# A fused attention and mixture kernel on one core: sums over keys brought into token order by overlapping tiles and a block transpose on VectorE, with other edits

## The chip, the cores and the metric

The kernel runs on one core of a Trainium2 chip. The metric is device time in microseconds, the median of several runs of the whole program; lower is better.

## The reference

Three stages follow each other. Attention over 4 batches of 8 heads with 1152 keys and 64 columns a head; the queries are first averaged in pairs, so that 576 are left:

```python
q_pool = q.reshape(B, H, S // 2, 2, D).mean(axis=3)
attn = softmax(q_pool @ k.T / sqrt(D))          # over the 1152 keys
x = (attn @ v)                                  # 2304 tokens x 512
```

Then a soft mixture of 8 experts with 4 slots each, and at the end a two-layer block:

```python
logits = x @ phi                                # 2304 x 32
d = softmax(logits, over tokens); c = softmax(logits, over slots)
slot_out[e] = relu((d.T @ x)[e] @ w1[e]) @ w2[e]
x = c @ slot_out
h = x @ w_in
out = piecewise(h) @ w_out     # h above 1, (h+1)^2/4 between, 0 below -1
```

## The kernel before

**Attention.** Two heads are worked on together, which makes 16 pairs (P, `NP`), four to a batch. The keys of a pair are 9 chunks of 128 (`NK`). A step g is one chunk of one pair (g = 9 P + c), and each step has two halves, h = 0 and 1, one for each head. In one half the loop at the end of the attention part issues, in this order:

- `max_half`: scores of another pair, 11 chunks ahead, with the queries on the partitions (tile `mx`, 4 matmuls in float16, L297), of which VectorE takes the largest (L309).
- `st`: the scores of this chunk with the keys on the partitions (tile `st`, 4 matmuls with `K` and 4 with `S`, L363), of which ScalarE takes the exponential (tile `e`, L368).
- at the first half of some steps, what `pre` holds: `es_sum` of the pair that has just ended (L387), and before it `t_pe` of an older pair (L422, L430).
- `pv`: values times exponentials of the chunk before, 4 matmuls in float32 instructions (tile `acc`, L394).
- `slot(g, h)`: whatever the schedule `sched` holds for this half: sums, evictions, preparation of later pairs, conversion of weights.

`mx`, `st` and the tiles of the steps in token order (`tx`, `lt`, `lr`, `pb`) share one ring of three PSUM buffers (`sc_tile`, tag `sc`). A matmul into a buffer waits until the last reader of what the buffer held is done: VectorE if that was an `mx`, ScalarE if it was an `st`.

**The sums over keys.** `es_add` adds the exponentials of chunks 0 to 5 on VectorE (L376, whole 128x576 tiles or half ones, by the table `ADD`: half-step, chunk, head, first and last part). `es_sum` then multiplies the sum and the chunks 6 to 8 with a column of ones repeated 32 times, into free columns of `acc`, in columns 0 to 191 and 192 to 287 of each query half. At b + 9 (b = 9 P) `t_raw` and `t_sum` copy `acc` to `xT` and the sums to `sq` on ScalarE.

**Token order.** Nine steps later (g0 = b + 18) `t_x` brings a pair's result into token order: 40 matmuls of 96 columns multiply 32 tokens of `xT` with `tab`, which holds an identity and the columns of phi, so that 64 columns of x and 32 of logits come out. The 576 tokens are five tiles of 128, of which the last repeats 64 tokens (`TC`). `t_rec` brings the sums into the same order with 20 more matmuls of 2 columns, `t_fin` (L444, L446) makes reciprocals of them out of PSUM, `t_ev` (L439) copies x and logits to `XL`, and ten `t_mul` (L450, by the table `TML`) multiply each tile of each head. After the fourth pair of a batch the logits are added over heads (`lg_red`, L468), their maximum is taken over tokens (`lg_mx`, `lg_tr`, `lg_max`, `lg_rep`), exponentials are made (`lg_exp`) and `p_mm` multiplies them with x (tile `pb`). The last pair does all this at once after its last step, in `t_last` and the list behind it in `plan`.

**Queues and order.** `plan` writes what is done in which half of which step; tables of numbers set it (`ADD`, `TML`, `CVS` for the four steps of a weight conversion, `PREP` for preparing K and queries of a later pair: the sixth number is the half-step of `prep_qlo`, L275, the low parts of the queries). All DMAs are issued by SyncE, in program order. `w_load` fetches an expert weight of 1 MB with one DMA: one in 9 steps from step 21 on, at steps with g % 9 = 3, and more at the end as pools are closed. The last of them (`w_last`) takes the place of `XL` after `p_mm`.

**The rest.** The experts (`h1`, `s2o`, limited by these weights and TensorE), the softmax over slots with its transposes (`c_xpose`), and the two-layer block with tile `po` (L965). None of the tables reaches into the last block.

Of the kernel before, what the change touches and what calls it, by code (L numbers as in the profile page):

```python
# [38 lines left out]
PREP = (-20, -18, (-34, -33), -36, -16, -30), (-24, -22, (-37, -36), -37, -17, -34)  # L39
# [3 lines left out]
def fused_kernel(ctx: ExitStack, tc: tile.TileContext, q, k, v, phi, w1, w2, w_in, w_out, out):  # L43
# [11 lines left out]
    TC = tuple(min(128 * t, TQ - 128) for t in range((TQ + 127) // 128))  # L55
    NTT = len(TC)
# [375 lines left out]

    def t_pe(P):
        t_x(P, range(NTT))
        t_rec(P)

    def t_ev(P):
        for h in range(2):
            nc.scalar.activation(out=XL[:, :, 2 * (P % HPB) + h, :], in_=tx[P][:, h, 0:NTT * BW].rearrange("p (t d) -> p t d", t=NTT),  # L439
# [687 lines left out]
```

## Time and profile before

| | us |
|---|---|
| median of 3 runs | 798.60 |
| lowest, highest | 798.33, 799.05 |
| the profiled run, its own time | 797.23 |
| span of the profiled run, first to last instruction | 795.4 |
| TensorE busy in the span | 740.0 (93%) |
| VectorE busy | 585.8 (74%) |
| ScalarE busy | 460.2 (58%) |
| DMA queue of SyncE, share of 16 engines | 55.7% |

Busy time of TensorE is modelled, since its matmuls overlap; a half with many short matmuls counts as busy throughout. Attention takes the span from about 13 to 511 us, the steps behind its last chunk run to 525 us, the experts to 560 us, the two-layer block to the end. A wait is shown in brackets behind the instruction that ended it, with the instruction waited for.

### The profile page before, as it was taken

To read this page: it belongs to the slowest core of one execution; us is meant where nothing else is said; L and a number is where in the kernel's file an instruction comes from. 1 tells how busy PE (TensorE), PEld (TensorE's weight loads), DVE (VectorE), ACT (ScalarE), POOL (GpSimd) and SP (SyncE) were. 2 spreads that over 40 slices of the span, in tenths; PEclk is the share of its full clock that TensorE was granted. 3 is DMA by queue.
4 is the path that set the end of the run, shared out by engine and by line. 5 is a ranking of instruction groups with operands and counts; after the bars stand their busy time and mean duration, and the time that the engine had idled before them with its cause. 6 is when DMAs were issued, how large, how long until landed. Compare 5 with 4: busy or idle time off the path is not lost.

```text
span 795.4 us, 21850 instructions
## 1 busy us (share of the span) xinstructions
PE 740.0 (93%) x9290; PEld 581.5 (73%) x9290; DVE 585.8 (74%) x1052; ACT 460.2 (58%) x882; POOL 107.9 (14%) x78
## 2 busy tenths in 40 slices
PE   7789999998999998999998899869999999999998
PEld 6567787786787786777786687533678888888887
DVE  6889788788697788697797584652556788888542
ACT  4256657655567656566655366510688767767550
POOL 7000000000000000000000000001243433434440
PEclk9899999999999999999999999999999999999999
DMA  9597769866559759369669516699300220310122
GB/s 214 121 221 158 147 172 221 181 155 190 99 149 245 150 159 223 60 183 209 164 161 208 173 47 225 210 388 375 156 1 16 91 80 27 97 64 1 53 93 93
DMA packets 134353, 118.89 MB, mean 149 GB/s; under 512 B 80240, under 2 KB 98928, under 8 KB 133744
## 3 DMA queue, kind: packets, MB, share of 16 engines
q1 hardware_dynamic: 134256, 117.50, 55.7%
q8 instruction: 73, 1.20, 0.6%
q14 instruction: 24, 0.20, 0.1%
HBM read 82.90 MB, written 8.91 MB: 115 GB/s over the span
## 4 chain that ended last, share of the span: by engine, by line
PE 65%; DVE 16%; DMA 7%; ACT 6%; issue 5%; SPq 1%; ACTq 0%; DVEq 0%
PE po L965 24%; PE st L363 12%; PE acc L394 9%; DVE mp L309 7%; PE mx L297 5%; DVE es L376 5%; PE acc L387 3%; PE tx L422 3%; DMA f<-in_moe_w_in_dram 2%; PE h L901 2%; ACT e L368 2%; ACT xl L450 2%; PE s2o L773 2%; PE h L720 1%; DMA S<-K 1%
## 5 line engine op out<-in xcount | busy, mean ns | idle before, releaser
L368 ACT ACTIVATE e<-st 128x576 f32<-128x576 f32 x288 | 187.0, 650 | 147.2 <-PE st L363 131.5
L309 DVE TENSOR_REDUCE mp<-mx 128x1 f32<-128x576 f32 x282 | 210.1, 751 | 56.1 <-PE mx L297 54.6
L394 PE MATMUL acc<-e,vf 128*64 128x288 f32 x1152 | 204.0, 411 | 3.5 <-ACT e L368 3.5
L363 PE MATMUL st<-q,K 128*64 128x288 f16 x1152 | 132.0, 289 | 16.0 <-ACT e L368 12.9
L297 PE MATMUL mx<-K,q 128*64 128x288 f16 x1152 | 127.3, 293 | 10.9 <-DVE mp L309 4.2
L363 PE MATMUL st<-q,S 128*64 128x288 f16 x1152 | 132.0, 287 | 1.4 <-DMA q<-qn 1.4
L297 PEld LDWEIGHTS <-q 128*64 128x64 f16 x1152 | 79.0, 111 | 64.6 <-issue 15.8
L965 PE MATMUL po<-whi,ghi 128*128 128x512 f32 x280 | 109.8, 392 | 0.0
L965 PE MATMUL po<-wlo,ghi 128*128 128x512 f32 x280 | 109.6, 392 | 0.0
L965 PE MATMUL po<-whi,glo 128*128 128x512 f32 x280 | 109.3, 390 | 0.0
L363 PEld LDWEIGHTS <-K 128*64 128x64 f16 x1152 | 76.3, 109 | 38.6 <-issue 33.5
L376 DVE TENSOR_TENSOR es<-es,e 128x288 f32<-128x288 f32 (+1 forms) x175 | 102.6, 593 | 0.0
L934 POOL TENSOR_TENSOR glo<-r,ghi 128x1024 fp32r<-128x1024 f32 x34 | 81.8, 2406 | 117.8 <-DVE r L922 75.8
L394 PEld LDWEIGHTS acc<-e,vf 128*64 128x64 f32 x1152 | 84.9, 137 | 9.0 <-ACT e L368 6.1
L363 PEld LDWEIGHTS <-S 128*64 128x64 f16 x1152 | 77.9, 110 | 2.5 <-issue 1.6
L699 POOL MEMSET xT<- 128x1024 f32 x1 | 1.0, 957 | 495.4 <-PE tx L422 495.4
L977 DVE TENSOR_TENSOR pa<-po,pa 128x512 f32<-128x512 f32 (+1 forms) x54 | 36.8, 681 | 39.7 <-PE po L965 39.7
L965 PEld LDWEIGHTS po<-whi,glo 128*128 128x128 f32 x280 | 52.6, 188 | 11.7
L965 PEld LDWEIGHTS po<-whi,ghi 128*128 128x128 f32 x280 | 52.6, 188 | 10.9 <-issue 0.4
L965 PEld LDWEIGHTS po<-wlo,ghi 128*128 128x128 f32 x280 | 52.6, 188 | 10.2
L922 DVE SCALAR_TENSOR_TENSOR r<-h,cl 128x512 f32<-128x512 f32 x68 | 43.6, 682 | 10.1 <-ACT cl L918 7.7
L450 ACT ACTIVATE xl<-xl,ss 128x96 f32<-128x96 f32 x150 | 45.9, 367 | 0.0
(184 smaller groups left out, 863.5 us busy)
## 6 DMA issues: line engine op xcount, KB each, us to landing
w<-in_moe_w_dram SPq DMA_DIRECT2D x31, 1024.0 KB, 7.5
vf<-in_v_dram SPq DMA_DIRECT2D x16, 576.0 KB, 5.4
kf<-in_k_dram SPq DMA_DIRECT2D x30, 288.0 KB, 3.8
f<-in_moe_w_in_dram SPq DMA_DIRECT2D x16, 512.0 KB, 4.4
f<-in_moe_w_out_dram SPq DMA_DIRECT2D x16, 512.0 KB, 3.7
qf<-in_q_dram SPq DMA_DIRECT2D x30, 256.0 KB, 4.6
S<-K SPq DMA_DIRECT2D x16, 288.0 KB, 5.8
out_dram<-pa SPq DMA_DIRECT2D x17, 256.0 KB, 2.0
```

The costliest lines, as they stand in the source:

```text
L297: nc.tensor.matmul(ps[p0:p1, i, 0:HQ], lhsT=q1[P][:, t, p0:p1], rhs=kk[:, j * HQ:(j + 1) * HQ], start=True, stop=True)
L309: nc.vector.tensor_reduce(out=mp[P][:, t, a:a + 1], in_=ps[:, :, 0:HQ], op=ALU.max, axis=AX.XY)
L363: nc.tensor.matmul(ps[c0:c0 + 64, i, 0:HQ], lhsT=kk[:, ci, c0:c0 + 64], rhs=f[:, sl[i]], start=first, stop=not first)
L368: nc.scalar.activation(out=e, in_=ps[:, :, 0:HQ], func=AF.Exp, scale=ESC)
L376: nc.vector.tensor_tensor(out=Es[P, n, h][:, i0:i1], in0=a[:, i0:i1], in1=b[:, i0:i1], op=ALU.add)
L387: nc.tensor.matmul(acc[P, i][32 * j:32 * j + 32, HQ:HQ + c1 - c0], lhsT=ones.to_broadcast([128, 32]), rhs=src[:, j % 2, c0:c1], start=Fals ...
L394: nc.tensor.matmul(acc[P, i][h * 64:(h + 1) * 64, 0:HQ], lhsT=vt[P][:, h, c, :], rhs=E[P, c, h][:, i, :], start=(c == 0), stop=(c == NK - ...
L450: nc.scalar.activation(out=x, in_=x, func=AF.Copy, scale=ss[P][:, t, h:h + 1])
L922: nc.vector.scalar_tensor_tensor(out=r[:, a:a + 2], in0=ps[a // 2], scalar=-1.0, in1=cl[:, a:a + 2], op0=ALU.max, op1=ALU.add)
L934: nc.gpsimd.tensor_tensor(out=glo[k], in0=r, in1=ghi[k].bitcast(F32), op=ALU.subtract)
L965: nc.tensor.matmul(ps, lhsT=a, rhs=b, start=st_, stop=sp)
L977: nc.vector.tensor_tensor(out=t, in0=po, in1=t, op=ALU.add)
```

## The change

It has these parts.

1. **Tiles of tokens overlap.** The five tiles begin at 0, 112, 224, 336 and 448 (`TS` = 112), each with 128 tokens, so that the first 16 of tiles 1 to 4 repeat tokens (`DUP`). `es_sum` reads its exponentials with that stride, so that the sums of 32 tokens stand in one block of 32 columns: 32 matmuls of 160 columns a pair in place of 32 of 192 or 96. Repeated tokens get -1e30 in `lg_exp`.
2. **Block transpose.** `t_sum` copies the sums (two pieces of 160 columns) into the dead tile `Es`, and `t_fin` turns it on VectorE in blocks of 32x32 (one instruction of 128x320), adds 1e-9 and takes the reciprocal. It stands at b + 10, not behind `t_x`; `t_rec` and its 20 matmuls are gone, and `tx` has no reader on VectorE.
3. **Fewer products in token order.** `t_x` takes both heads in one matmul of 192 columns for tiles 0 to 3: 24 matmuls a pair, not 40. `XL` is laid out by pair, so that `lg_red` is three reductions, in three halves, not two.
4. **Tables.** `TML` puts two `t_mul` in each of five halves from g0 + 3 half-steps on (before: four at one half, then two in each of three). `prep_qlo` of pairs from 3 on is two half-steps later. `ADD` moves some sums and cuts one more in two. `CVS`: the four conversion steps of a pair now stand in its first three halves; pairs 10 to 12 do three, pairs 5, 9 and 13 none.
5. **The last pair.** `t_last` adds the logits of each tile and head with ten instructions in place of one and two `lg_add`; x is scaled by six ScalarE and four VectorE instructions in place of five and one.
6. **Weights.** While the attention part is written, `w_load` puts four quarters of 256 KB in a list, and one (in the last 8 steps two) is issued at the end of each step.
7. **Transposes of the softmax over slots.** `c_first` turns the first tile of all batches, `c_xpose` four tiles a batch: 20 transposes as before, 5 evictions in place of 8.

The core of the diff:

```diff
-CVS = ((0, 0), (0, 1), (1, 1), (8, 1)), ()
+CVS = ((0, 0), (0, 0), (0, 1), (1, 1)), ((0, 0), (0, 0), (0, 1)), ()
-TML = (2, 0, 0), (2, 1, 0), (2, 0, 1), (2, 1, 1), (3, 0, 2), (3, 1, 2), (4, 0, 3), (4, 1, 3), (5, 0, 4), (5, 1, 4)
+TML = (3, 0, 0), (3, 0, 1), (4, 1, 0), (4, 1, 1), (5, 0, 2), (5, 0, 3), (6, 1, 2), (6, 1, 3), (7, 0, 4), (7, 1, 4)
-PREP = (-20, -18, (-34, -33), -36, -16, -30), (-24, -22, (-37, -36), -37, -17, -34)
+PREP = (-20, -18, (-34, -33), -36, -16, -30), (-24, -22, (-37, -36), -37, -17, -32)
...
     def es_sum(P):
...
+            for h in range(2):
+                src = (E[P, grp[n][0], h] if n else Es[P, 0, h])
+                for r in range(4):
+                    a = src.rearrange("p i n -> p (i n)")[:, 32 * r:32 * r + 32]
+                    a = bass.AP(tensor=a.tensor, offset=a.offset, ap=[a.ap[0], [TS, NTT], [1, 32]])
+                    nc.tensor.matmul(acc[P, h][32 * r:32 * r + 32, HQ:HQ + SW], lhsT=ones.to_broadcast([128, 32]),
+                                     rhs=a, start=False, stop=False, skip_group_check=True)
...
+    def t_fin(P):
+        es = Es[P, 0, 0].rearrange("p i n -> p (i n)")
+        nc.vector.transpose(out=sq, in_=es[:, 0:2 * SW])
+        ss[P] = g4.tile([128, 2, NTT], F32, tag="ss", bufs=2, name=f"ss{P}")
+        nc.vector.tensor_scalar(out=ss[P], in0=sq.rearrange("p (h t z) -> p h t z", h=2, z=32)[:, :, :, 0],
+                                scalar1=1e-9, scalar2=None, op0=ALU.add)
+        nc.vector.reciprocal(out=ss[P], in_=ss[P])
...
         for t in ts:
-            for h in range(2):
+            for hs in ((0, 2),) if t < 4 else ((0, 1), (1, 2)):
+                i, k = place(t, hs[0])
                 for r in range(4):
-                    c0 = TC[t] + 32 * r
-                    nc.tensor.matmul(tx[P][32 * r:32 * r + 32, h, BW * t:BW * t + BW], lhsT=xT[:, P % 2, c0:c0 + 32],
-                                     rhs=tab[:, P % HPB, h, :], start=True, stop=True)
+                    c0 = TS * t + 32 * r
+                    nc.tensor.matmul(tx[P][32 * r:32 * r + 32, i, BW * k:BW * (k + hs[1] - hs[0])], lhsT=xT[:, P % 2, c0:c0 + 32],
+                                     rhs=tab[:, P % HPB, hs[0]:hs[1], :], start=True, stop=True)
-    def t_rec(P):
...
+                if part == 0:
+                    x = LG[:, NTT * (P // HPB) + t, :]
+                    nc.vector.scalar_tensor_tensor(out=x, in0=px(h, t)[:, D:BW], scalar=sc, in1=x, op0=ALU.mult, op1=ALU.add)
...
-            for s, f, *a in ((8, lg_red, 0, 3, H), (9, lg_red, 3, 5, H), (9, lg_mx), (10, lg_tr), (12, lg_max), (13, lg_rep),
-                             (14, lg_exp), (16, p_mm), (17, p_add)):
+            for s, f, *a in ((7, lg_red, 0, HPB), (8, lg_red, 1, HPB), (9, lg_red, 2, HPB), (9, lg_mx), (11, lg_tr), (11, lg_max), (13, lg_rep),
+                             (13, lg_exp), (16, p_mm), (16, p_add)):
...
+            wq.extend((vw[:, c], src[:, c]) for c in range(4))
...
+            w_piece(1 + (g > nsteps - NK))
```

What this moves, at three places in pair 7 (the names end in the pair, the chunk and the head; `st7_2_1` is the score tile of pair 7, chunk 2, head 1).

On TensorE, the first matmul into `mx8_4_1` and `st7_2_1` with the engine whose semaphore it waits for, before:

```order
L297 MATMUL mx8_4_1_4005<-K1_8_3439,q1_8_3492 64x288 [waits DVE_49]
L297 LDWEIGHTS q1_8_3492
...
L297 MATMUL mx8_4_1_4005<-K1_8_3439,q1_8_3492 64x288
L363 LDWEIGHTS K1_7_2899
L363 MATMUL st7_2_1_4011<-q1_7_2951,K1_7_2899 64x288 [waits Activation_49]
```

and with the change:

```order
L311 MATMUL mx8_4_1_3824<-K1_8_3289,q1_8_3341 64x288 [waits PE_49]
L311 LDWEIGHTS q1_8_3341
...
L311 MATMUL mx8_4_1_3824<-K1_8_3289,q1_8_3341 64x288
L377 LDWEIGHTS K1_7_2777
L377 MATMUL st7_2_1_3830<-q1_7_2826,K1_7_2777 64x288 [waits DVE_49]
```

The buffer of the score tile was last read by ScalarE before, and is last read by VectorE now. Before, five score tiles of pair 7 wait in this way for ScalarE (`st7_2_0` to `st7_4_0`); with the change none does.

On ScalarE, from the exponential of chunk 1, head 0, of pair 7 on, before:

```order
L368 ACTIVATE e7_1_0_3941<-st7_1_0_3932 128x576 [waits PE_49,Activation_49]
L450 ACTIVATE xl_109<-xl_109,ss5_3919 128x96 [waits DVE_49,Activation_49]
L450 ACTIVATE xl_109<-xl_109,ss5_3919 128x96 [waits Activation_49]
L450 ACTIVATE xl_109<-xl_109,ss5_3919 128x96 x2
L268 ACTIVATE qn1_108<-qf9_3539 128x9x64 [waits DMAHW3_49,DMAHW2_49,DMAHW5_49,DMAHW1_49,DMAHW0_49]
L368 ACTIVATE e7_1_1_3969<-st7_1_1_3960 128x576 [waits PE_49]
```

and with the change:

```order
L382 ACTIVATE e7_1_0_3760<-st7_1_0_3751 128x576 [waits PE_49,Activation_49]
L282 ACTIVATE qn1_110<-qf9_3393 128x9x64 [waits DMAHW3_49,DMAHW6_49,DMAHW1_49,DMAHW7_49,DMAHW0_49,DVE_49]
L382 ACTIVATE e7_1_1_3787<-st7_1_1_3778 128x576 [waits PE_49,Activation_49]
L462 ACTIVATE xl_111<-xl_111,ss5_3286 128x96 [waits Activation_49]
L462 ACTIVATE xl_111<-xl_111,ss5_3286 128x96
L382 ACTIVATE e7_2_0_3815<-st7_2_0_3806 128x576 [waits PE_49]
```

Between these two exponentials stood four `t_mul` and the high parts of the queries; now the high parts stand there alone.

On VectorE, from the reduction of `mx8_2_1` on, behind the block of sums of pair 6, before:

```order
L309 TENSOR_REDUCE mp8_3696<-mx8_2_1_3900 128x1 [waits PE_49]
L444 TENSOR_SCALAR ss5_3919<-tx5_3799 128x10 [waits Activation_49]
L446 RECIPROCAL ss5_3919<-ss5_3919 128x10 [waits DVE_49]
L195 TENSOR_SCALAR wst1_73<-wst1_73 128x512
L309 TENSOR_REDUCE mp8_3696<-mx8_3_0_3926 128x1 [waits PE_49]
L275 SCALAR_TENSOR_TENSOR qn2_1_107<-qf9_3539,qn1_108 128x9x64 [waits DMAHW6_49,Activation_49]
L309 TENSOR_REDUCE mp8_3696<-mx8_3_1_3954 128x1 [waits PE_49]
```

and with the change:

```order
L323 TENSOR_REDUCE mp8_3556<-mx8_2_1_3722 128x1 [waits PE_49]
L212 SCALAR_TENSOR_TENSOR wst1_73<-f64_1_75,wst1_73 128x512 [waits DVE_49]
L323 TENSOR_REDUCE mp8_3556<-mx8_3_0_3745 128x1 [waits PE_49]
L432 STREAM_TRANSPOSE xT_112<-es6_0_0_3365 128x320 [waits Activation_49]
L434 TENSOR_SCALAR ss6_3766<-xT_112 128x10 [waits DVE_49]
L436 RECIPROCAL ss6_3766<-ss6_3766 128x10 [waits DVE_49]
L323 TENSOR_REDUCE mp8_3556<-mx8_3_1_3772 128x1 [waits PE_49]
L215 SCALAR_TENSOR_TENSOR wst1_73<-f64_1_75,wst1_73 128x512
L323 TENSOR_REDUCE mp8_3556<-mx8_4_0_3800 128x1 [waits PE_49]
L289 SCALAR_TENSOR_TENSOR qn2_1_109<-qf9_3393,qn1_110 128x9x64 [waits DMAHW6_49,Activation_49]
```

The reciprocals are now those of pair 6, not 5, made from the transposed sums; the low parts of the queries stand two reductions later; the conversion steps have come forward.

## Rows read from the trace of the kernel before

**Rows 1.** Stretches: length, busy time and count of each engine, clock, DMA share, GB/s.
```profile
85.24:449.73 364.49, 342.33 (x5793) 272.38 (x5791) 300.43 (x532) 222.10 (x457) 0.00 (x0) 1.00 0.73 173
114.23:142.93 28.70, 27.52 (x475) 22.43 (x473) 24.26 (x44) 18.61 (x39) 0.00 (x0) 1.00 0.77 185
171.62:206.82 35.20, 32.19 (x516) 24.03 (x515) 27.51 (x49) 18.88 (x39) 0.00 (x0) 0.95 0.65 153
449.73:511.20 61.47, 53.43 (x968) 43.44 (x966) 39.02 (x72) 37.18 (x84) 0.00 (x0) 0.97 0.46 153
```
**Rows 2.** Timeline of pair 7's first half: start, us, engine, line, operation, count [idle before].
```profile
264.29 0.44 PE L363 MATMUL st<-q,K 128*64 128x288 f16 x4
264.90 1.86 PE L422 MATMUL tx<-tab,xT 128*32 128x96 f32 x80
266.57 0.49 PE L430 MATMUL tx<-ident,xT 128*32 128x2 f32 x38
266.94 0.68 PE L387 MATMUL acc<-es,cols 128*32 128x192 f32 x14
269.01 0.71 PE L394 MATMUL acc<-e,vf 128*64 128x288 f32 x4
269.79 0.41 PE L363 MATMUL st<-q,K 128*64 128x288 f16 x4
270.00 0.76 DVE L309 TENSOR_REDUCE mp<-mx 128x1 f32<-128x576 f32 x1 [2.16 <-PE mx L297]
```
**Rows 3.** Timeline, the third to fifth half behind it.
```profile
272.28 0.44 PE L363 MATMUL st<-q,K 128*64 128x288 f16 x4
272.38 1.16 ACT L450 ACTIVATE xl<-xl,ss 128x96 f32<-128x96 f32 x4
273.45 0.67 ACT L268 ACTIVATE qn<-qf 128x576 f16<-128x576 f32 x1
274.15 0.76 DVE L275 SCALAR_TENSOR_TENSOR qn<-qf,qn 128x576 f16<-128x576 f32 x1 [2.10 <-ACT qn L268]
274.70 0.44 PE L363 MATMUL st<-q,K 128*64 128x288 f16 x4 [1.01 <-ACT e L368]
275.42 0.65 ACT L368 ACTIVATE e<-st 128x576 f32<-128x576 f32 x1 [0.24 <-PE st L363]
276.12 0.44 PE L363 MATMUL st<-q,K 128*64 128x288 f16 x4
```
**Rows 4.** Timeline, VectorE and score matmuls later in pair 7.
```profile
286.39 0.45 DVE L376 TENSOR_TENSOR es<-es,e 128x288 f32<-128x288 f32 x1
286.52 0.44 PE L363 MATMUL st<-q,K 128*64 128x288 f16 x4
286.75 0.75 DVE L309 TENSOR_REDUCE mp<-mx 128x1 f32<-128x576 f32 x1
...
287.74 0.44 PE L363 MATMUL st<-q,K 128*64 128x288 f16 x4
287.82 0.75 DVE L376 TENSOR_TENSOR es<-es,e 128x576 f32<-128x576 f32 x1
288.49 0.75 DVE L309 TENSOR_REDUCE mp<-mx 128x1 f32<-128x576 f32 x1
289.29 0.44 PE L363 MATMUL st<-q,K 128*64 128x288 f16 x4
```
**Rows 5.** Timeline at a batch's end (pair 8).
```profile
313.07 1.04 DVE L468 TENSOR_REDUCE xT<-xl 128x64 f32<-128x512 f32 x1
```
**Rows 6.** Timeline between pairs 13 and 15: waits of TensorE.
```profile
455.66 0.24 PE L387 MATMUL acc<-es,cols 128*32 128x96 f32 x1 [3.23 <-issue]
499.29 0.46 PE L394 MATMUL acc<-e,vf 128*64 128x288 f32 x1 [1.45 <-ACT e L368]
```
**Rows 7.** Timeline behind the last pair: two products of 512 columns, and a wait.
```profile
521.96 1.07 PE L505 MATMUL pb<-xl,xT 128*32 128x512 f32 x8
...
533.45 1.07 PE L720 MATMUL h<-w_last,xT 128*32 128x512 f32 x8 [3.70 <-DMA w_last<-in_moe_w_dram]
```

More of the change, by code (lines that the diff above doesn't have):

```diff
@@ L54, in fused_kernel @@
     HPB = H // 2
-    TC = tuple(min(128 * t, TQ - 128) for t in range((TQ + 127) // 128))
-    NTT = len(TC)
+    NTT = (TQ + 127) // 128
+    TS = (TQ - 128) // (NTT - 1)
+    DUP = 128 - TS
+    SW = NTT * 32
     BW = D + NS
@@ L107, in fused_kernel, with w_piece @@
     nloaded, gone = 0, set()
+    wq = []
+    def w_piece(n):
+        for _ in range(min(n, len(wq))):
+            o, i = wq.pop(0)
+            nc.sync.dma_start(out=o, in_=i)
     def w_load():
@@ L433, in t_pe @@
[L433 to L437, printed above, removed]
-        for h in range(2):
-            nc.scalar.activation(out=XL[:, :, 2 * (P % HPB) + h, :], in_=tx[P][:, h, 0:NTT * BW].rearrange("p (t d) -> p t d", t=NTT),
-                                 func=AF.Copy)
-    def t_fin(P):
-        ss[P] = g4.tile([128, NTT, 2], F32, tag="ss", name=f"ss{P}")
-        nc.vector.tensor_scalar(out=ss[P], in0=tx[P][:, 1, NTT * BW:NTT * BW + 2 * NTT].rearrange("p (t h) -> p t h", h=2),
-                                scalar1=1e-9, scalar2=None, op0=ALU.add)
-        nc.vector.reciprocal(out=ss[P], in_=ss[P])
@@ L475, in lg_mx, with lg_red @@
+    bt = {}
+    def lg_red(b, i, n):
+        if i < 2:
+            x = XL[:, 0:n, NTT * i:NTT * i + 4, D:BW].rearrange("p c (u h) s -> p u s c h", u=2)
+            o = LG[:, NTT * b + 2 * i:NTT * b + 2 * i + 2, :]
+        else:
+            x = XL[:, 0:n, 4:2 * NTT:NTT, D:BW].rearrange("p c h s -> p s c h")
+            o = LG[:, NTT * b + 4, :]
+        nc.vector.tensor_reduce(out=o, in_=x, op=ALU.add, axis=AX.XY)
     def lg_mx(b):
@@ L566, in plan @@
         g0 = b + (11 if P == NP - 2 else 18)
-        pre.setdefault((g0, 0), []).insert(0, (t_pe, P))
-        at(g0, 0, t_ev, P)
-        at(g0, 1, t_fin, P)
+        pre.setdefault((g0, 0), []).insert(0, (t_x, P, range(NTT)))
+        for i in range(2):
+            at(g0, 0, t_ev, P, i)
+        at(b + 10, 0, t_fin, P)
         for c, h, t in TML:
@@ L753, in c_soft, with c_first @@
                 nc.vector.tensor_tensor(out=CN[:, :, r + 1, :], in0=lgN, in1=CN[:, :, r, :], op=ALU.subtract)
+        def c_first():
+            ps = hp_tile("cf")
+            for b in range(B):
+                nc.tensor.transpose(out=ps[:, b * 128:(b + 1) * 128], in_=CN[:, NTT * b].rearrange("p r s -> p (r s)"), identity=ident)
+            nc.scalar.activation(out=cT.rearrange("p (b n) -> p b n", b=B)[:, :, 0:128],
+                                 in_=ps.rearrange("p (b n) -> p b n", b=B), func=AF.Copy)
         def c_xpose(b):
```

120 lines of the change are left out of this document (56 added, 64 removed).

## The prediction, on record before the changed kernel ran

> **What bounds the kernel now.** I read the stretches first, to see which part of the span has room. From 85 to 450 us TensorE passes twelve times from one pair's token-order products to the next (the first row of [rows 1]): 364.49 us, with TensorE busy for 342, VectorE for 300 and ScalarE for 222. Nine of these cycles are plain and three hold a batch's end. A plain one takes 28.70 us, the same to 0.01 us from pair to pair, and a batch's end about 35 (the second and third of [rows 1]). Nothing in a plain cycle is full: VectorE is busy for 24.26 of 28.70. So the question is what each of its 18 halves waits for, and for that I read the timeline of one cycle.
>
> An undisturbed half is 1.22 us, from one `st` to the next (286.52 to 287.74, [rows 4]). The half with the products and sums takes 5.50, from 264.29 to 269.79 [rows 2]. Eighteen halves would be 17 x 1.22 + 5.50 = 26.2 us; the cycle has 2.5 more, and three things make them:
>
> - ScalarE is late once a cycle. Between two exponentials stand four `t_mul` (1.16 together) and the high parts of the queries (0.67), and the half takes 2.42 in place of 1.22, with TensorE idle for 1.01 [rows 3]. That is 1.20 lost.
> - Then the ring of PSUM buffers is out of step. The score matmul at 276.12 starts when the exponential of the half before, 275.42 + 0.65, is done, so the half takes 1.42 [rows 3]. Four halves do so: 0.80 lost.
> - VectorE is late in the rest. A reduction begins 0.21 after its `st` when VectorE is free (the last two of [rows 2]), and the next `st` starts 0.80 after the reduction began (288.49 to 289.29, [rows 4]). So VectorE may be 0.21 late at no cost; beyond that TensorE waits. At 289.29 it has lost 0.33; two more halves lose 0.05 each.
>
> From 450 to 511 us the last pairs run with little reduction work, but TensorE idles there for other reasons [rows 6]; its granted clock is 0.97 of full over that stretch and 0.95 in the first batch's end [rows 1], which is some 3.4 us at the lower level, 1.2 GHz, in each. Behind the last pair the chain ends on the transfer of `w_last` [rows 7]. The experts and the two-layer block, from 535 us on, are TensorE work that the change leaves alone.
>
> **The change part by part.**
>
> *TensorE.* `t_rec` goes: the sums start at 266.94 instead of 266.57 [rows 2], so 0.4 a pair. `t_x` has fewer instructions but the same columns (16 x 192 + 8 x 96 = 40 x 96), and 80 recorded matmuls took 264.90 to 266.57, 0.022 us each for 96 columns. The sums, 64 recorded matmuls of 144 columns on average, took from 266.94 to 269.01, 0.032 each: about as much a column. So columns are the cost: nothing for `t_x`, and 160 columns in place of 144 add 0.23. The half becomes 5.50 - 0.40 + 0.23 = 5.33. This gain alone is 0.17 a pair.
>
> *ScalarE.* `t_mul` costs 0.29 apiece [rows 3]. With two in a half, an exponential of 0.65 and two of them fit into 1.22; the high parts of the queries stand alone (0.65 + 0.67 = 1.32, with 0.08 less for each instruction, because starts overlap by that much: the half sum, 0.45 long, is followed after 0.36 [rows 4]). So the 1.20 go.
>
> *The ring.* In the new order every `st` of a plain cycle waits for VectorE, none for ScalarE, since `tx` is now released by ScalarE in its own half. The 0.80 go. What is late next is VectorE, since each half then leaves it 1.22 and not 1.42.
>
> *VectorE.* The block transpose is not in the trace. The nearest row is the half sum, 288 elements in 0.45 [rows 4]; 32 elements more at the slope between it and the whole sum (0.75 for 576) make 0.48, and the whole sum, 0.75, is the upper end, since one pass over 320 elements should not exceed one over 576. I take 0.48, the nearer. With the two small instructions the `t_fin` group takes some 0.8 from reduction to reduction, of which 0.4 is new. I then add up VectorE's work in the new order from start to start: 0.67 for a reduction or a whole sum (287.82 to 288.49, [rows 4]), 0.36 for a half sum. The 17 halves behind the block hold, in order, 1.27, 1.45, 1.27, 1.36, 1.34, 1.34, 1.04, 1.41, 1.04, 1.34, 1.34, 1.04, 1.81, 1.04, 1.34, 1.34, 1.34 = 22.1 us, where TensorE would take 17 x 1.22 = 20.7. VectorE is therefore the bound there by 1.4, less 0.2 that it may run late for nothing and a little that it finishes in the block. Carried from half to half this gives 1.1 us of waiting, 0.4 of it at the half with 1.81. A plain cycle becomes 20.7 + 5.3 + 1.1 = **27.2 us**. Its ends: 26.1, if VectorE keeps up; 28.1, if the three waits go and VectorE gives 2.0 back, as with a transpose of 0.75 and small instructions dearer than rows of before.
>
> The Trainium skill (VectorE: DVE Perf Modes, The three transpose paths) gives 311 ns for a VectorE transpose of 128x128 in bf16 and says that it works in 32x32 blocks only. No run here shows one yet; scaled with the 0.96 GHz of that page, 320 columns would be an estimate of 0.51, and the plain cycle the same to 0.05 us.
>
> *Batch ends.* `lg_red` in three halves: two reductions of 512 elements at 1.04 [rows 5] and one of half that. Added up in the same way VectorE has 25.5 us of work in 17 halves, and `lt`, `lr` and `pb` add some 2 us to TensorE, part of it while VectorE catches up. Block, halves, VectorE's 5.3 beyond TensorE and 1.6 of these products: 33.0 us, against 34.7 as the mean of the three (35.20 is one of them).
>
> The twelve cycles: 9 x 27.2 + 3 x 33.0 = 343.8 against 364.5: **20.7 less**.
>
> *The end, 450 to 511 us.* A wait of 3.23 with no releaser, 1.45 for an exponential behind four `t_mul` [rows 6], and 0.03 of 61.5 us lost to the clock (1.8): 6.5 at stake. The first has no cause in view; the second is what `TML` mends. I take half, **3.3 less**; ends 0 and 8.
>
> *At nothing.* Two memsets at the start stand behind a DMA that TensorE waits for. Pair 0 keeps its ring, and in pair 1 three waits for ScalarE (0.6) give way to the new work on VectorE. Ten small sums behind the last pair cost VectorE up to 1 us more, the missing `t_rec` 0.5 less; and the transfer of `w_last` ends later than either [rows 7]: if that cover were gone, 1 us. `c_first`: three evictions less in 5 us of matmuls. More quarters on SyncE's queue stand in front of later loads and transposes, one in each step of two halves, in place of four at once.
>
> Sum: 20.7 + 3.3 = 24.0 from the profiled run's 797.2, that is 773.2. The median lies 1.4 above the profiled run, so **774**. Less than 0.2% (1.6 us) could not be told from no change.
>
> **The rivals.**
>
> *VectorE gives most of it back* (12%). For it: work of 22.1 in 20.7. The Trainium skill (VectorE: DVE Perf Modes, Rules for kernel authors) says to minimize the count of instructions, which speaks against a change that adds some forty; the trace agrees in that two half sums (0.90) cost more than a whole one (0.75). Against: the busy sum of a plain cycle rises only from 24.3 to 24.8. Then 28.1 a plain cycle, 9 x 0.6 = 5.4, 1 from batch ends, 2 from the end: 790.
>
> *VectorE keeps up* (8%). 26.1 a plain cycle, 9 from batch ends, 7 from the end: 9 x 2.6 + 16 = 39 less, 759.
>
> *Quarters make the transposes late* (6%). The engines of the queue are 0.77 busy in a plain cycle at 185 GB/s [rows 1], so a quarter now lies beside the transposes of the next queries, where one load lay ahead of them. If `st` or `mx` waits 2 us for them in each of 12 pairs, the gain is gone: 798. Against it: the only wait of this kind in a plain cycle before is none. The Trainium skill (DMA: Bandwidth & Descriptors, Bandwidth) says to batch transfers to 1 MiB or more; by it quarters keep the queue busy for longer, which no run here shows yet.
>
> *The strided reading of the sums is slow* (5%), and the kernel becomes slower. `es_sum` reads blocks of 32 columns at a distance of 112 over each other; at half rate the sums take 2 x 2.3 and 16 pairs lose 37 us against the forecast: 811. It decides from about 1.5 us more a pair, 3.8 for the sums. Against it: `p_mm` reads blocks of 64 columns and its products take as long as ones of 512 in a row, 1.07 for eight [rows 7].
>
> **How the numbers follow.** The forecast has 69%. The range takes in the first rival and its own ends (plain cycles from 26.3 to 28.1): 762 to 790; the second, and those at 798 and 811, are left out, 8 + 11%. Faster: 69 + 12 + 8 and a third of the DMA rival, 91%; same 3%; slower 6%.
>
> **What would show it.** Plain cycles, from `tx` to `tx`, of 27 us; no half of 2.4 behind them and no runs of 1.42; waits of `st` named VectorE; VectorE over 0.9 busy there; a transpose row near 0.48; the sums near 2.3 us. A transpose above 0.75, cycles above 28.2, or waits on `q` or `K` transfers in each pair would prove it wrong.

## The result, and the profile after

The changed kernel takes **768.3 us** (median of 4 runs, 766.85 to 769.94), the kernel before beside it 798.5: a ratio of 0.9625, 95% interval 0.9602 to 0.9648. The prediction was 774 (762 to 790), faster with 0.91. The profiled run took 767.93, its span is 766.2, so 29.2 us of span are gone. I split them at the starts of `tx` that the prediction used:

| stretch | before | after | difference | predicted |
|---|---|---|---|---|
| up to the first `tx` | 85.24 | 85.80 | +0.6 | 0 |
| twelve cycles | 364.49 | 341.08 | -23.4 | -20.7 |
| the last three pairs, to the last `tx` | 64.68 | 54.53 | -10.2 | -3.3 |
| behind the last `tx` | 281.0 | 284.8 | +3.8 | 0 |

Each stretch comes from one profiled run. Other kernels below share the program behind the last `tx` with one of the two: that of before took 281.0 to 282.9 us there in five kernels, that of the change 282.6 to 285.0 in five. So the +3.8 is the upper end of a spread, and the means differ by 1.6. The twelve cycles and the last three pairs differ by far more than such a spread.

The stretches of the changed kernel (columns as in [rows 1]): the twelve cycles, a plain one, a batch's end, the last three pairs, and from the last `tx` to the first use of `w_last`, for which TensorE waits.

```profile
85.80:426.88 341.08, 331.67 (x4929) 261.46 (x4927) 304.17 (x558) 222.30 (x457) 0.00 (x0) 1.00 0.75 175
112.86:139.93 27.07, 26.86 (x403) 21.66 (x401) 24.77 (x47) 18.70 (x39) 0.00 (x0) 1.00 0.82 196
166.99:198.86 31.87, 30.09 (x445) 22.24 (x443) 26.78 (x52) 19.08 (x39) 0.00 (x0) 1.00 0.57 143
426.88:481.41 54.53, 53.16 (x804) 41.38 (x804) 42.13 (x79) 39.03 (x88) 0.00 (x0) 1.00 0.66 211
...
481.41:503.43 22.02, 16.51 (x151) 9.30 (x151) 10.14 (x34) 2.70 (x9) 1.21 (x2) 0.69 1.02 361
```

A plain cycle is 27.06 where [rows 1] had 28.70. VectorE does 24.8 us of work in it as foretold, now 0.92 of the time. The granted clock is 1.00 from the first to the last `tx` and 0.69 from there to the use of `w_last`, where the kernel before had 1.00.

The view of waits groups TensorE's waits by who ended them (us in total, times, longest). Over the twelve cycles of the kernel before:

```profile
PE st L363 <- ACT e L368: 12.1, 12, 1.0
PE lt L481 <- DVE xT L476: 4.4, 3, 1.5
...
PE st L363 <- DVE mp L309: 0.7, 3, 0.2
```

and of the changed kernel:

```profile
PE st L377 <- DVE mp L323: 5.1, 14, 0.6
PE mx L311 <- DMA q<-q: 1.5, 1, 1.5
PE lt L497 <- DVE mp L323: 1.1, 3, 0.4
PE st L377 <- ACT e L382: 0.4, 1, 0.4
```

The twelve waits of 1.0 for ScalarE, one in each cycle, are gone, and waits for VectorE have taken their place: 5.1 us where ScalarE had 12.1. A batch's end no longer waits 1.5 us for its maximum; this I had not counted.

The timeline of the changed kernel, the half with the products and sums, and the block transpose behind it (the rows that answer to [rows 2]):

```profile
279.43 0.44 PE L377 MATMUL st<-q,K 128*64 128x288 f16 x4
...
280.04 1.84 PE L449 MATMUL tx<-tab,xT 128*32 128x192 f32 x48
...
281.69 0.73 PE L402 MATMUL acc<-es,cols 128*32 128x160 f32 x16
...
282.24 1.81 PE L402 MATMUL acc<-e,cols 128*32 128x160 f32 x48
...
283.98 0.71 PE L409 MATMUL acc<-e,vf 128*64 128x288 f32 x4
...
284.76 0.42 PE L377 MATMUL st<-q,K 128*64 128x288 f16 x4
...
286.87 0.50 DVE L432 STREAM_TRANSPOSE xT<-es 128x320 f32<-128x320 f32 x1
...
287.40 0.17 DVE L434 TENSOR_SCALAR ss<-xT 128x10 f32<-128x10 f32 x1
...
287.61 0.22 DVE L436 RECIPROCAL ss<-ss 128x10 f32<-128x10 f32 x1
```

From `st` to `st` this half takes 5.33, the number of the prediction; the sums, from 281.69 to 283.98, 2.29. The transpose takes 0.50 (predicted 0.48).

Late in a plain cycle of the changed kernel (the place of [rows 4]), VectorE is the one that is waited for:

```profile
247.04 0.44 PE L377 MATMUL st<-q,K 128*64 128x288 f16 x4
247.12 0.82 DVE L390 TENSOR_TENSOR es<-es,e 128x288 f32<-128x288 f32 x2
247.86 0.75 DVE L323 TENSOR_REDUCE mp<-mx 128x1 f32<-128x576 f32 x1
...
248.67 0.44 PE L377 MATMUL st<-q,K 128*64 128x288 f16 x4 [0.21 <-DVE mp L323]
```

This is the half with 1.81 us of work on VectorE; it takes 1.63, that is 0.41 lost (the account said 0.4).

Behind the last pair, the timeline of the changed kernel (against [rows 7]):

```profile
483.32 1.68 DVE L474 SCALAR_TENSOR_TENSOR xT<-tx,ss,xT 128x32 f32<-128x32 f32 x10 [0.51 <-PE tx L449]
...
485.51 0.43 PE L497 MATMUL lt<-ident,mx 128*32 128x128 f32 x8 [1.62 <-DVE mx L492]
...
486.46 0.86 DVE L478 TENSOR_SCALAR xl<-tx,ss 128x64 f32<-128x64 f32 x4 [1.01 <-ACT xl L476]
487.24 0.28 DVE L501 TENSOR_REDUCE cols<-lt 128x1 f32<-128x128 f32 x1
...
490.74 1.94 PE L524 MATMUL pb<-xl,xT 128*32 128x512 f32 x8
...
493.27 0.37 SPq L137 DMA_DIRECT2D w_last<-in_moe_w_dram  x1
...
503.43 1.06 PE L741 MATMUL h<-w_last,xT 128*32 128x512 f32 x8 [1.04 <-DMA w_last<-in_moe_w_dram]
```

`lt` is there at 485.5, but the maximum over it (L501) stands behind four scalings, which wait for ScalarE. TensorE idles, its clock falls to the lower level (1.2 GHz), and the products of `pb` take 1.94 where [rows 7] have 1.07. The stretch behind that fall, with the clock at 0.50 of full:

```profile
488.00:500.00 12.00, 10.35 (x68) 6.04 (x72) 4.04 (x9) 1.11 (x3) 0.00 (x0) 0.50 1.05 389
```

`w_last` is asked for 11.9 us behind the start of `tx`, 9.1 before.

### The profile page after: what moved, and what is told of

Its sections match the earlier page's. It is cut to its first block, busy times and chain, and to the rows that moved or that the text cites. A ratio compares the mean times of both kernels' runs of the same rounds, so it can differ in the third digit from the quotient of the medians.

```text
span 766.2 us, 19663 instructions
## 1 busy us (share of the span) xinstructions
PE 731.4 (95%) x8138; PEld 569.4 (74%) x8138; DVE 595.4 (78%) x1104; ACT 460.9 (60%) x880; POOL 108.0 (14%) x78
## 4 chain that ended last, share of the span: by engine, by line
PE 58%; DVE 30%; issue 5%; DMA 4%; ACT 2%; SPq 1%; DVEq 0%; ACTq 0%
PE po L991 25%; DVE mp L323 12%; DVE es L390 10%; PE st L377 7%; PE acc L409 6%; PE acc L402 5%; PE tx L449 4%; PE mx L311 3%; PE h L927 2%; PE s2o L798 2%; PE h L741 1%; DMA q<-q 1%; DMA w_last<-in_moe_w_dram 1%; DVE qn L289 1%; DVE xT L489 1%
## 5 line engine op out<-in xcount | busy, mean ns | idle before, releaser
L409 PE MATMUL acc<-e,vf 128*64 128x288 f32 x1152 | 201.4, 408 | 1.6 <-ACT e L382 1.6
L311 PE MATMUL mx<-K,q 128*64 128x288 f16 x1152 | 125.6, 291 | 11.2 <-DVE mp L323 4.3
L377 PE MATMUL st<-q,K 128*64 128x288 f16 x1152 | 129.3, 288 | 7.4 <-DVE mp L323 5.5
L377 PE MATMUL st<-q,S 128*64 128x288 f16 x1152 | 129.4, 286 | 0.1
L311 PEld LDWEIGHTS <-q 128*64 128x64 f16 x1152 | 76.4, 111 | 64.4 <-issue 8.3
L377 PEld LDWEIGHTS <-K 128*64 128x64 f16 x1152 | 74.4, 109 | 26.5 <-issue 16.1
L409 PEld LDWEIGHTS acc<-e,vf 128*64 128x64 f32 x1152 | 82.9, 137 | 9.3 <-ACT e L382 4.4
L377 PEld LDWEIGHTS <-S 128*64 128x64 f16 x1152 | 75.9, 110 | 1.3 <-issue 0.4
L991 PEld LDWEIGHTS po<-wlo,ghi 128*128 128x128 f32 x280 | 52.9, 189 | 10.2
```

What stands on the lines that cost most here:

```text
L311: nc.tensor.matmul(ps[p0:p1, i, 0:HQ], lhsT=q1[P][:, t, p0:p1], rhs=kk[:, j * HQ:(j + 1) * HQ], start=True, stop=True)
L377: nc.tensor.matmul(ps[c0:c0 + 64, i, 0:HQ], lhsT=kk[:, ci, c0:c0 + 64], rhs=f[:, sl[i]], start=first, stop=not first)
L409: nc.tensor.matmul(acc[P, i][h * 64:(h + 1) * 64, 0:HQ], lhsT=vt[P][:, h, c, :], rhs=E[P, c, h][:, i, :], start=(c == 0), stop=(c == NK - ...
L991: nc.tensor.matmul(ps, lhsT=a, rhs=b, start=st_, stop=sp)
```

## The experiments

All cycles below are from `tx` to `tx` in the timeline of one profiled run. Medians are from different rounds, in which the kernel before took 798.5 to 801.7 us, so totals compare by their ratios to it. The changed kernel has 0.960 to 0.965; of the eight variants of it below only `a_last` lies clear of that, so what the others are worth is read from cycles and stretches.

### The two tables alone, on the kernel before

```diff
 b_tml:    TML as in the change (ss with a second buffer)
 b_qlo:    -PREP ... (-24, -22, (-37, -36), -37, -17, -34)
           +PREP ... (-24, -22, (-37, -36), -37, -17, -32)
 b_tmlqlo: both
```

> The kernel before with one edit: TML as in the change (two t_mul in each of five halves; the reciprocals get a second buffer, which the later products need). ScalarE theory (mine): the half of 2.42 us behind four t_mul goes to 1.24, and in the order three score tiles of pair 7, not five, still wait for ScalarE, so of the 0.80 of the ring some 0.4 stays: a plain cycle 28.70 - 1.2 - 0.4 = 27.1 us, VectorE taking up to 0.3 of it, so 27.1 to 27.4; twelve cycles 16 to 19 us less and 1.4 at the end, total 778 to 782. Rival (VectorE takes its place): plain cycles of 28.2 or more, total above 792.

> The kernel before with one edit: the low parts of the queries (prep_qlo) two half-steps later. In the order this alone takes the waits of score tiles for ScalarE from five to one in pair 7, although tx is still read by VectorE in the next half; so what sets the ring would be the place of prep_qlo and not the reader of tx. Ring theory: three halves of 1.42 go to 1.22 (0.6 to 0.8 a cycle), the half of 2.42 stays: plain cycle 27.9 to 28.1 us, total 789 to 792. Rival (the ring is a symptom of late ScalarE, its 0.8 is not to be had alone): 28.5 or more, total above 796. Rival (VectorE's wait of 2.10 for the high parts in front of prep_qlo costs by itself): plain cycle below 27.5.

> The kernel before with both of these edits, and without the block transpose. If the two are worth 1.20 and 0.80 a cycle and VectorE gives back under 0.4: plain cycles 26.8 to 27.2 us, total 774 to 779, so that these two tables carry nearly all of the gain of the twelve cycles and the block transpose about nothing. If the block transpose, the fewer products and the earlier conversion steps carry a part of their own: plain cycles above 27.6, total above 784.

| kernel | plain cycle | twelve cycles | end | median, us | ratio, 95% |
|---|---|---|---|---|---|
| before | 28.70 | 364.5 | 64.7 | 800.0 | |
| b_tml | 27.50 | 350.4 | 66.3 | 788.6 | 0.981 to 0.989 |
| b_qlo | 27.64 | 353.2 | 66.1 | 789.2 | 0.981 to 0.988 |
| b_tmlqlo | 26.91 | 345.1 | 66.9 | 782.1 | 0.974 to 0.980 |
| after | 27.06 | 341.1 | 54.5 | 768.3 | 0.960 to 0.965 |

The halves of the cycle of pair 7, from one `st` to the next (the first is the one with products and sums):

```
before    5.50 1.26 1.22 2.42 1.42 1.42 1.42 1.42 1.22 1.22 1.22 1.22 1.27 1.22 1.55 ...
b_tml     5.50 1.27 1.22 1.48 1.42 1.42 1.23 1.33 1.22 1.22 1.22 1.22 1.27 1.21 1.56 ...
b_qlo     5.50 1.26 1.22 1.22 1.48 1.90 1.22 1.22 1.22 1.22 1.22 1.22 1.27 1.22 1.55 ...
b_tmlqlo  5.50 1.26 1.22 1.22 1.22 1.42 1.22 1.23 1.22 1.22 1.22 1.22 1.27 1.22 1.55 ...
after     5.33 1.22 1.22 1.34 1.27 1.33 1.33 1.33 1.22 1.22 1.22 1.22 1.27 1.22 1.62 ...
```

The two tables together carry all of a plain cycle's gain and a little more: 1.79 of 1.64. The rest of the change wins 0.17 in the first half and gives 0.3 back behind it, where VectorE now also transposes; sums and conversion steps were moved there too, and which of these it is was not tried. What the rest does win in the twelve cycles is the ends of batches: 33.3 to 33.7 us in `b_tmlqlo`, 31.9 to 32.3 in the changed kernel, 4.2 in all for the three, where the twelve cycles differ by 4.0. The two do not add up (1.20 + 1.06 against 1.79): the 2.42 is gone with either, though `b_qlo` has a half of 1.90 two places on. And `b_qlo` has no runs of 1.42 although `tx` is read by VectorE as before, so the new reader of `tx`, which the prediction named as the cause, is not needed for it. Whether that reader would do it alone was not tried.

`b_tml` and `b_tmlqlo` came out above their expected totals (778 to 782, 774 to 779): the end did not shrink but grew, by 1.4 to 2.2 in the three kernels, and in `b_tml` the twelve cycles won 14.1 where 16 to 19 were expected. `b_qlo` met its total, with a plain cycle shorter than its 27.9 to 28.1.

### The two tables undone, or VectorE burdened, in the changed kernel

```diff
 a_tml:  TML as before
 a_dve2: +        for _ in range(2):
              nc.vector.transpose(out=sq, in_=es[:, 0:2 * SW])
 a_pool: -        eng = nc.gpsimd if P == 1 else nc.vector
         +        eng = nc.gpsimd if P >= 1 else nc.vector
```

> The changed kernel with one part undone: TML as before (four t_mul at one half, two in each of three). In the order no score tile waits for ScalarE in pairs 6, 7 and 10, so the ring stays in step. ScalarE theory: one half of each cycle becomes about 2.4 us long again; since VectorE is behind by about 1.0 us a cycle in the changed kernel, which that pause lets it make up, the plain cycle grows from 27.06 by 0.4 to 1.2: 27.5 to 28.3, total 774 to 784. Rival (with the queries' low parts later, late ScalarE costs nothing): plain cycle below 27.2, total below 770.

> The changed kernel with the block transpose done twice into the same place (0.50 us more of VectorE's work a pair, starting 0.43 after the one before). VectorE is the bound (prediction): a plain cycle grows by 0.4 to 0.5, twelve cycles by 5 to 6, total 773 to 776; in the order three score tiles of pair 7 then wait for ScalarE, which may add up to 0.6 a cycle (total up to 781). Rival (TensorE is the bound and VectorE has slack): below 0.15 a cycle, total below 771.

> The changed kernel with 0.67 us a pair taken off VectorE: the sum of neighbouring queries (prep_qp) of pairs 2 to 15 goes to GpSimd, which is idle in attention and took 1.77 us for it in pair 1. VectorE is the bound: the plain cycle goes from 27.06 to between 26.3 and 26.6 (26.1 is TensorE alone), twelve cycles 5 to 8 us less, total 760 to 764. Rival 1 (TensorE is the bound): 768 +- 1.5. Rival 2 (GpSimd at work slows VectorE, or the queries come late): 770 or more, VectorE's reductions longer than 0.75 us beside it.

`a_tml`: 773.1 us (ratio 0.962 to 0.971), a plain cycle 27.31, only 0.25 more; the expectation of 0.4 to 1.2 was too high. With the ring in step a late exponential holds up the next product with `vf` (its weight loads wait 10.1 us for `e` in all, 4.4 in the changed kernel) and not the score matmul, and most of the 1.16 us of four `t_mul` is absorbed. So late ScalarE has no price of its own: undoing it is worth 1.20 with the ring out of step (`before` to `b_tml`), 0.73 in the kernel before with the ring in step (`b_qlo` to `b_tmlqlo`), and 0.25 in the changed kernel, where VectorE is behind as well; that it makes up for lost time in the pause is argued, not shown.

`a_dve2`: 772.8 us (0.962 to 0.969), a plain cycle 27.59, 0.53 more for this row of VectorE (L433 is its line of the transpose):

```profile
236.79 1.05 DVE L433 STREAM_TRANSPOSE xT<-es 128x320 f32<-128x320 f32 x2
```

VectorE is the bound at that place: what is added shows in full. In the cycle from 257.51 three score matmuls behind it do start right after an exponential, as the order foretold, but VectorE works on without a gap, and the next one, at 270.49, starts when VectorE's reduction (269.68 + 0.75) is done.

`a_pool`: 774.5 us (0.962 to 0.971), no gain, with plain cycles of 27.5 to 28.0, slower than the 27.06 of the changed kernel. GpSimd takes 1.41 for the sum, and this happens beside it:

```profile
247.45 0.75 DVE L323 TENSOR_REDUCE mp<-mx 128x1 f32<-128x576 f32 x1
247.64 1.41 POOL L279 TENSOR_TENSOR qf<-qf 128x576 f32<-128x576 f32 x1 [26.31 <-DVE es L390]
248.23 0.85 DVE L356 TENSOR_TENSOR mm<-mp 128x9 f32<-128x9 f32 x1
...
250.73 0.44 PE L377 MATMUL st<-q,K 128*64 128x288 f16 x4 [0.89 <-DVE mp L323]
```

The reduction, whose one input is in PSUM, takes its 0.75; the small maximum over `mp`, with two inputs in SBUF, takes 0.85 in place of 0.17 and ends with GpSimd's instruction (249.08 and 249.05). Rival 2 holds in that GpSimd slows VectorE, but not by its sign, the reductions. TensorE then waits 0.89 in place of 0.21.

### Weights in quarters

```diff
 b_quart: the list of quarters of the change, on the kernel before
 a_whole: the changed kernel with w_load as before, 1 MB and one a step at most
```

> The kernel before with one edit: weights in quarters of 256 KB, one a step (two in the last eight). Theory of the prediction: nothing (795 to 800). Rival: the wait of 3.23 us with no releaser in the end stretch of before is TensorE's fetch of instructions standing behind a load of 1 MB (the instruction queue moves two packets in those 9 us, beside a load that takes 300 to 400 GB/s); quarters leave gaps, the wait goes and the transfers of queries are no longer late: 3 to 5 us less, 793 to 796, all of it between 450 and 515 us. Rival (quarters make transposes late): above 801.

> The changed kernel with one part undone: weights loaded whole, one of 1 MB a step at most, as before. Prediction's theory: nothing, 767 to 770. Rival 1 (the end stretch is better by 10 us because quarters leave gaps for the fetch of instructions and for transposes): the wait without releaser behind the products of pair 13 comes back with 3 us or more, the end stretch grows from 54.5 to 58 or more, total 772 or more. Rival 2 (quarters cost): the one wait of 1.55 us for a transfer of queries in pair 11's cycle (29.02 instead of 26.7) goes, total 765 to 767.

`a_whole` takes 769.1 us (0.957 to 0.966), end 55.1, tail 285.0: whole loads do as well as quarters in the changed kernel. `b_quart` takes 797.8 (0.994 to 0.998): 0.4% less, where the rival had 3 to 5 us. Its end shows why it is little. TensorE's waits there, `b_quart`:

```profile
456.08 0.24 PE L397 MATMUL acc<-es,cols 128*32 128x96 f32 x1 [1.49 <-issue]
480.05 0.44 PE L373 MATMUL st<-q,S 128*64 128x288 f16 x4 [1.25 <-DMA q<-qn]
488.03 0.31 PE L373 MATMUL st<-q,S 128*64 128x288 f16 x1 [2.32 <-issue]
```

and in `b_tmlqlo`, with whole loads:

```profile
437.19 0.32 PE L387 MATMUL acc<-es,cols 128*32 128x96 f32 x1 [4.17 <-issue]
463.87 0.44 PE L363 MATMUL st<-q,S 128*64 128x288 f16 x4 [1.45 <-DMA q<-qn]
```

The wait without releaser, 3.23 in the kernel before, halves with quarters, and another of 2.32 appears. Neither wait is in the changed kernel, with quarters or whole. The late transfer of pair 11 (1.55 in the changed kernel) is 1.51 in `a_whole`, so quarters do not make it either.

### The tail

```diff
 a_tail:  -WARM = 2, 2, 3, 2, 6, 3
          +WARM = 6, 2, 3, 2, 6, 3
          -(t_last, P, 2), (lg_max, q_), (lg_rep, q_), (warm, WARM[1]), (lg_exp, q_), (warm, WARM[2]),
          +(lg_max, q_), (lg_rep, q_), (warm, WARM[1]), (lg_exp, q_), (t_last, P, 2), (warm, WARM[2]),
 a_wlast: h1(1, 0) behind h1(5, 0), h1(6, 0), h1(7, 0)
 a_best:  both
 a_last:  a_tail, and h1(1, 0) with c_soft behind h1(5, 1)
```

`h1(e, x)` is the product with the expert weight (e, x), and (1, 0) is `w_last`; `WARM` counts small matmuls whose result nothing reads.

> The changed kernel with two edits behind the last pair: the maximum, its replication and the exponential stand in front of the four scalings of x on VectorE, and 12 instead of 4 small matmuls follow the token-order products (WARM[0] 6, not 2). Clock theory: TensorE's clock stays at 2.4 GHz from 487 to 501 us (row PEclk 1.0 there), the product of exponentials and x ends 9.2 us behind the start of tx in place of 11.8, w_last is asked for 2.6 us earlier and lands 2 to 2.6 earlier: the tail behind the last tx 284.8 -> 282.2 us, total 765 to 767. Rival (the DMA queue is full until w_last lands, so it lands no earlier): w_last lands 22 us behind tx as now, tail within 0.5 of 284.8, total 768 +- 1.

> The changed kernel with one edit: the first expert product of w_last comes last of its eight, behind those of experts 5 to 7 (3.1 us of matmuls). If TensorE's wait for w_last is all that its transfer costs (1.04 us in the changed kernel): tail 284.8 -> 283.7, total 767.2. If w_last sets the end by more than the wait shows: 1.5 to 3 less. Rival (the softmax over slots, which begins later by 3 us, becomes late in front of its transposes): no gain or a loss.

> Both edits of the tail together. Clock theory with w_last out of the way: the product of exponentials and x ends 2.6 us earlier, the expert products run at full clock from there and wait for nothing, or for w_last by less than 1: tail 284.8 -> 280.5 to 281.5, total 764 to 765. If w_last lands 22 us behind tx whatever the clock does: 3.1 us of matmuls ahead of its wait give 281.5 to 283. If the rival of the softmax holds: above 283.5.

> The changed kernel with the two edits of the tail (maximum first, 12 small matmuls) and w_last's product moved behind thirteen other expert products instead of three or seven (11.8 us of matmuls at full clock). Bandwidth theory: w_last lands 22 us behind the last tx again, whatever TensorE does, but TensorE has matmuls until then, waits under 0.5 us for it and keeps its full clock; the expert products end some 3 us earlier than in the kernel with the w_last edit alone, unless the weights behind w_last (8 of 1 MB, 2.7 us each at 387 GB/s, so the last lands some 44 us behind tx) set the end instead. Tail 279.5 to 282 us, total 761 to 766. Rival (those last weights do set the end): tail 281 to 282.5 and waits for w in the second expert stage. Rival (softmax over slots late): above 283.

| kernel | behind the last `tx` | `w_last` used at, from `tx` | median, us | ratio, 95% |
|---|---|---|---|---|
| after | 284.8 | 22.0 | 768.3 | 0.960 to 0.965 |
| a_tail | 285.1 | 21.5 | 768.7 | 0.957 to 0.963 |
| a_wlast | 281.3 | 22.2 | 766.5 | 0.955 to 0.964 |
| a_best | 283.3 | 21.9 | 768.8 | 0.957 to 0.964 |
| a_last | 280.8 | 24.0 | 765.4 | 0.952 to 0.959 |

These tails stand against the 282.6 to 285.0 of the five kernels with the changed program there, so only `a_wlast` and `a_last` lie below that spread.

`a_tail` does to the clock what it should, and wins nothing. Its stretches (columns as above) and what stands at their edge:

```profile
486.30:498.30 12.00, 8.93 (x98) 5.02 (x98) 6.73 (x18) 2.28 (x8) 0.00 (x0) 1.00 1.03 385
498.30:503.68 5.38, 0.00 (x1) 0.01 (x1) 0.00 (x0) 0.00 (x0) 0.00 (x0) 0.82 1.05 387
503.68:511.68 8.00, 8.00 (x52) 2.02 (x56) 2.55 (x4) 0.60 (x1) 0.31 (x1) 0.69 1.05 384
```

```profile
503.68 1.94 PE L741 MATMUL h<-w_last,xT 128*32 128x512 f32 x8 [6.79 <-DMA w_last<-in_moe_w_dram]
```

TensorE is done early at full clock, waits 6.79 us for `w_last`, and the clock falls in that wait, so that the products behind it run at 0.69 on average. The bandwidth rival holds: the DMA engines are full (1.03 and more), and though `w_last` is asked for 3.4 us sooner it lands after as many bytes as in the changed kernel (21.48 us at 370 GB/s, 22.02 at 361: 7.9 MB each).

`a_wlast` takes the wait out of the way. Its products, and its stretch from the last `tx` to `w_last`:

```profile
495.59 7.91 PE L741 MATMUL h<-w,xT 128*32 128x512 f32 x56 [0.45 <-DVE xT L735]
503.32 1.04 PE L741 MATMUL h<-w_last,xT 128*32 128x512 f32 x8
```

```profile
481.10:503.32 22.22, 18.14 (x174) 9.74 (x178) 10.14 (x34) 2.70 (x9) 1.21 (x2) 0.77 1.02 368
```

Its tail is 3.5 us shorter than in the profiled run of the changed kernel, and 1.3 to 3.7 shorter than in the five kernels; the expectations were 1.04, or 1.5 to 3. `w_last` is used as late as there (22.2), but three more expert products are done by then. The wait is 1.04 of that; for the rest the clock came back sooner in this run (0.77 over the stretch, 0.69 in the changed kernel). What brought it back sooner is open: up to these products the two programs are the same. The medians, 766.5 and 768.3, do not set the two kernels apart.

`a_best` falls between: starting earlier, it runs into the transfer again (a wait of 3.14) and loses its clock there; its 283.3 lies above the 283 that was expected at most, and under the 283.5 of the rival. `a_last`, with enough products ahead, has no wait for `w_last`; it gives some back behind it, where ScalarE and VectorE are late with what stood there before:

```profile
506.49 1.04 PE L741 MATMUL h<-w_last,xT 128*32 128x512 f32 x8
...
510.13 0.66 PE L750 MATMUL ht<-ident,Prun 128*128 128x128 f32 x4 [1.75 <-ACT Prun L828]
```

It is the fastest of all: 0.9552 of before (0.9518 to 0.9586), where the changed kernel has 0.9625, and its tail and median are as expected (279.5 to 282, 761 to 766).

## Why the prediction was right, and where it was not

- *What bounds the plain cycle*: right. The half of 2.42 and the runs of 1.42 are gone, the waits of `st` are named VectorE, and 27.06 stands against 27.2. `a_dve2` shows that VectorE is the bound behind the block.
- *TensorE's 0.17 a pair*: right to 0.01, and it is all that the products and sums are worth there.
- *ScalarE, 1.20*: the half of 2.42 is gone and `b_tml` wins 1.20 a cycle, but it is not a price of its own: 0.73 with the ring in step, 0.25 in the changed kernel (`a_tml`).
- *The ring, 0.80*: gone as said, but not for the reason given ("`tx` is now released by ScalarE in its own half"). The step that failed is that reason: `b_qlo` has the later low parts of the queries alone, with the old reader, and its runs of 1.42 are gone. It won 1.06 with them, and the other table on top of it 0.73. Why the place of the low parts changes whom a score tile waits for is open.
- *VectorE, 1.1 of waits*: 17 halves that would take 20.7 take 21.73, that is 1.0. The transpose at 0.50 lies by the lower end.
- *Batch ends, 33.0*: 32.1. The sum had no term for the wait of `lt` for its maximum, 1.5 before and 0.4 now. It also took VectorE as 5.3 beyond TensorE, where its own 25.5 and 20.7 differ by 4.8; so corrected it gives 32.4.
- *The end, 3.3 (0 to 8)*: mis-sized; 10.2 came. The wait without releaser (3.23) went whole, with the clock's 1.8 and a late transfer of 1.35. The sum left that transfer out, and a second wait for an exponential, 1.83 at 505.47, behind a weight conversion on ScalarE whose own data come late:

```profile
496.98 1.16 ACT L450 ACTIVATE xl<-xl,ss 128x96 f32<-128x96 f32 x4
...
504.21 0.66 ACT L186 ACTIVATE wst<-f 128x512 f32<-128x512 f32 x1 [1.78 <-DMA f<-in_moe_w_out_dram]
```

  Ahead of the wait of 1.45 at 499.29 four `t_mul` do stand (496.98), with a conversion behind them, but `TML` does not mend it: with `TML` moved, `b_tmlqlo` still waits 1.35 and 2.38 there, behind these rows of ScalarE:

```profile
479.70 0.66 ACT L186 ACTIVATE wst<-f 128x512 f32<-128x512 f32 x1 [0.78 <-DMA f<-in_moe_w_out_dram]
...
486.95 0.66 ACT L186 ACTIVATE wst<-f 128x512 f32<-128x512 f32 x1 [1.80 <-DMA f<-in_moe_w_out_dram]
```

  In the changed kernel the longest wait of a conversion for its data there is 0.25. Quarters are excluded as the cause of the shorter end (`a_whole`, 55.1), the two tables too (`b_tmlqlo`, 66.9). That the earlier conversion steps (`CVS`) do it is argued, not shown; why the wait without releaser went is open.
- *The tail, 0*: wrong by 3.8 in these two runs, by 1.6 in the mean of five kernels each. "`w_last` ends later than either" was right and decides it, but I took its landing as fixed. It lands 22.0 behind `tx` in place of 19.0 (18.3 to 19.4 in the five kernels with the old tail, 21.4 to 22.5 with the new one): 22.02 us at 361 GB/s are 7.9 MB between `tx` and its landing, where before it was 7.2 (19.04 at 378). The low clock, which looks like the cause, is not (`a_tail`). Nor is it that attention ends sooner: in `b_tmlqlo` the last `tx` starts 17.2 us sooner, and `w_last` lands 19.4 behind it. What differs is when the weights ahead of `w_last` are asked for. On SyncE's queue they stand behind the last write of a weight conversion (`cv_dr`) ahead of `tx`, and that comes 3.7 us ahead of `tx` in the kernel before (`tx` at 514.41) and 1.5 in the changed one (481.41):

```profile
510.69 0.33 SPq L204 DMA_DIRECT2D cv_dr<-wst  x1
...
511.58 8.77 SPq L125 DMA_DIRECT2D w<-in_moe_w_dram  x5
```

```profile
479.90 0.33 SPq L218 DMA_DIRECT2D cv_dr<-wst  x1
...
481.09 2.08 SPq L117 DMA_DIRECT2D w<-in_moe_w_dram  x4
```

  So these weights are asked for 2.8 us ahead of `tx` before and 0.3 with the change, also with whole loads (0.6 in `a_whole`) and, on the kernel before, with quarters (2.8 in `b_quart`). That the moved conversion steps put it there is argued; no run has them alone.
- *Rivals*: VectorE gave back 1.0 of 2.0 a cycle, as the forecast had it; quarters made nothing late; the strided sums show no loss of rate (2.29 for 160 columns in 64 matmuls, 2.07 for 144 on average before).
- *The total*: 5.7 us below the forecast (774, where its sum gives 774.6). The twelve cycles and the end won 2.7 and 6.9 more than said, the start and the tail lost 0.6 and 3.8. That the total lies so near is in part luck: the two errors of the end and the tail go against each other.

## What to carry to other kernels

Two waits that follow closely on each other need not have two prices: undo each alone and both together before adding them. In this kernel a low clock in front of a transfer that is late anyway cost nothing, and raising it only lengthened the wait, in which the clock fell again; look first at what the DMA engines still have to bring, and put work in front of it. Where a second engine is idle, look at what its instructions shut out before work is moved to it. Before two kernels are compared by the stretches of one profiled run, look how far a stretch varies between kernels that share its program.

## What the runs showed of the hardware that was not expected

- In `a_pool` GpSimd at work held up a VectorE instruction with two inputs in SBUF to its end (0.17 us became 0.85), and in another pair a small `TENSOR_SCALAR` with one input (L358, 0.19 became 1.28), but not a reduction, out of PSUM (0.75) or out of SBUF (L489 at 185.14, 0.59; 0.60 in the changed kernel). The Trainium skill (SBUF — State Buffer, Who interferes with whom) says that the two engines share a pair of ports under an exclusive lock, that a VectorE instruction with two SBUF inputs contends with a GpSimd instruction that reads SBUF, and that reductions don't; the trace agrees on both.
- TensorE waited 3.23 to 4.17 us without a releaser at one place, the same in `before`, `b_tml` (3.73), `b_qlo` (3.59) and `b_tmlqlo`, and one packet of the instruction queue (0.02 MB) moved within that wait. The Trainium skill (Runtime: NRT & Kernel Launch, Instruction fetch mechanics) says that an engine fetches its instructions in blocks of 16 KiB while it runs, mostly hidden; the packet has that size. That the wait is such a fetch, which is then not hidden here, is possible, and no run settles it: the waits without releaser of 1.49 and 2.32 in `b_quart` have no such packet inside.
